# Normalised attention and a snake feed-forward layer on one core: norm steps re-placed, the first batch re-staged, the rest key tile in array quadrants, last stores split

## The chip, the cores and the metric

One core of one Trainium2 chip runs the whole program. The metric is the device time of one execution in microseconds (us). It is read beside a profile of one execution, whose times are counted from that execution's first instruction.

## The reference

The inputs are q, k and v with 8 batches, 12 heads, 448 tokens and a head dimension of 64, two gains g_q and g_k of length 64, and a feed-forward layer with w_in (768 x 2048), w_out (2048 x 768) and alpha (2048). All are float32.

```python
q_n, k_n = rmsnorm(q, g_q), rmsnorm(k, g_k)          # over the head dimension, eps 1e-6
attn = softmax(q_n @ k_n.T / 8)                       # 448 x 448 for each batch and head
x = (attn @ v), heads side by side                    # 3584 tokens x 768
h = x @ w_in
g = h + sin(alpha * h)**2 / (alpha + 1e-9)
out = g @ w_out                                       # 3584 x 768
```

## The kernel before, in words

**Units of work.** A batch has 6 head pairs, head `hp` with head `hp + 6`, one in partitions 0 to 63 and one in 64 to 127 (`hi` 0 and 1). The index `pi` counts pairs through all batches. Norm works on chunks `ci` of two pairs, three to a batch and 24 in all. The 448 keys make three tiles of 128 and a rest tile of 64 (`t` = 0 to 3).

**Norm of a chunk** (`norm_tasks`, L150 to L223). The steps are: squares of q and k (L165 on ScalarE or L167 on GpSimd), the product of both gains folded into k (`fold_g`, L171), row sums on VectorE (L174), the inverse root by Ln and Exp on ScalarE (L178, L179), the scaling to bfloat16 (L189, L191, L196: five operations), and the transposes. The three chunks of batch 0 are "early": squares on ScalarE, transposes on TensorE into PSUM with a VectorE copy (L212, L213). All others use GpSimd for squares, fold and scaling, and a transposing DMA on SyncE's queue (L202). Only chunk 0 folds and scales on VectorE.

**Attention of a pair.** `scores(pi, t)` (L231) multiplies keys by queries for both heads, which sit in the two row halves of the array, and ScalarE takes the exponential (L243, L245). `attend(pi)` (L247) runs 16 matmuls (L262). For each key tile there are four: values for hi 0 and 1 into PSUM bank 0, and a tile of ones for hi 0 and 1, which gives the softmax sums, into bank 1. hi chooses the column half of the array in both banks; in the rest tile it chooses the row half as well:

```python
r = slice(hi * 64, hi * 64 + 64)
lhsT = vb[b][r, NT * H + hp, :] if bank == 0 else ones[r, :]
nc.tensor.matmul(av[r, bank, :S], lhsT, rhs, start=(t == 0), stop=(t == NT))
```

ScalarE then forms the reciprocal of the sums by Ln and Exp (L264, L265), and one VectorE product writes the pair's rows of xT (L268).

**Feed-forward.** `first_product(b)` (L286) is 16 row tiles of 6 matmuls (L293). The sine follows on ScalarE (L274), its square on GpSimd or ScalarE (L277, L279), and the sum on VectorE (L282). `second_product(b)` (L314) makes units of 16 steps, whose matmuls (L330) end in a VectorE copy (L335) and two stores on SyncE's queue (L340). Its steps are "fillers", run between the attention steps of the next batch; those of batch 7 run at the end.

**Order.** Nothing is reordered by a scheduler: each engine runs its instructions in the order in which Python issues them, and so does each DMA queue. In batch b's pair loop (L377) `bg(n)` (L227) takes the next n entries of the queue `background`, which holds the norm steps of chunks 3b+2 to 3b+4. What is left runs after `first_product` (L415).

**Buffers.** PSUM has four pairs of banks (`bank_pair`) for all products, three q/k chunk buffers (`inp`, L73) and two v buffers exist. `load_qk` (L90) fills a chunk from SyncE's queue, but chunks 1 and 2 come from ScalarE's queue (L116, L117). v, w_in and w_out are loaded with a cast by GpSimd (L104, L109, L140, L146); w_out and the v of batch 1 are issued after pair 2 of batch 0 (L406).

Of the kernel before, what the change touches and what calls it, by code (L numbers as in the profile page):

```python
# [23 lines left out]
BF16 = mybir.dt.bfloat16  # L24
# [7 lines left out]
def kernel(  # L32
# [33 lines left out]
    HALF = D_MODEL // 2  # L66

# [22 lines left out]
    def load_qk(ci, eng=nc.sync):  # L90

        b, dp = ci // NC, ci % NC
        qk[ci] = inp.tile([P, 2, 2 * NJ, D], F32, tag="qk", name="qk")
        for which, src in ((0, q), (1, k)):
            heads = src[b].rearrange("(hi dp pp) (p j) d -> dp (pp p) hi (j d)", hi=2, pp=2, j=NJ)[dp]
            eng.dma_start(out=qk[ci][:, which].rearrange("p (hi j) d -> p hi (j d)", hi=2), in_=heads)

    def load_v(b):


        vb[b] = vpool.tile([P, NT * H + NP, D], BF16, tag="vb", name="vb")
        tok = v[b].rearrange("h (p j) d -> p h (j d)", j=NJ)
        for jj in range(2):
            nc.gpsimd.dma_start(  # L104
                out=vb[b][jj * 64:jj * 64 + 64, :NT * H, :].rearrange("p (h t) d -> p h (t d)", t=NT),
                in_=tok[:, :, jj * NT * D:(jj + 1) * NT * D])
        last = v[b].rearrange("(hi pr) (p j) d -> j hi p pr d", hi=2, j=NJ)[NJ - 1]
        for hi in range(2):
            nc.gpsimd.dma_start(out=vb[b][hi * 64:hi * 64 + 64, NT * H:, :], in_=last[hi])  # L109
# [6 lines left out]
    load_qk(1, nc.scalar)  # L116
    load_qk(2, nc.scalar)  # L117
# [6 lines left out]
    nc.vector.memset(eps, 1e-6)  # L124
    gg = const.tile([P, 1, D], F32)
# [16 lines left out]
    def load_w_out():  # L142
        src = moe_w_out.rearrange("(mt p) d -> p mt d", p=P)
        for half in range(2):
            cols = slice(half * HALF, (half + 1) * HALF)
            nc.gpsimd.dma_start(out=w_out_sb[:, :, cols], in_=src[:, :, cols])  # L146
# [3 lines left out]
    def norm_tasks(ci):  # L150
# [8 lines left out]
        def square(w):  # L159
            if "ms" not in st:  # L160
                st["ms"] = npool.tile([P, 2, 2 * NJ], F32, tag="ms", name="ms")
                st["inv"] = npool.tile([P, 2, 2 * NJ], F32, tag="inv", name="inv")
            st[w] = npool.tile([P, 2 * NJ, D], F32, tag="sq", name="sq")
            if early:
                nc.scalar.activation(st[w], qk[ci][:, w], ACT.Square)  # L165
            else:
                nc.gpsimd.tensor_mul(st[w], qk[ci][:, w], qk[ci][:, w])  # L167

        def fold_g():
            eng = nc.vector if first else nc.gpsimd  # L170
            eng.tensor_mul(qk[ci][:, 1], qk[ci][:, 1], gg.to_broadcast([P, 2 * NJ, D]))  # L171
# [9 lines left out]
        def scale(w):  # L181
            eng = nc.vector if first else nc.gpsimd
# [12 lines left out]
            if w == 1:  # L195
                eng.tensor_mul(n[:, NJ - 1], x[:, :, NJ - 1], inv[:, :, NJ - 1].unsqueeze(2).to_broadcast([P, 2, D]))  # L196
# [18 lines left out]
        none = lambda: None  # L215
        if first:
            return [lambda: (square(0), reduce(0), rsqrt(slice(0, 1)), square(1), scale(0), reduce(1), fold_g(),
                             rsqrt(slice(1, 2)), scale(1)), lambda: pe_transpose(0), lambda: pe_transpose(1)]
        if early:
            return [lambda: (square(0), square(1), fold_g()), none, lambda: (reduce(0), reduce(1)), none,  # L220
                    lambda: (rsqrt(slice(0, 2)), scale(0), scale(1)), none, lambda: pe_transpose(0), lambda: pe_transpose(1)]
        return [lambda: (square(0), square(1), fold_g()), none, lambda: reduce(0), lambda: reduce(1),
                lambda: (rsqrt(slice(0, 2)), scale(0), scale(1)), none, none, transpose]  # L223

    background = deque()

    def bg(n):  # L227
        for _ in range(min(n, len(background))):
            background.popleft()()
# [17 lines left out]
    def attend(pi):  # L247

        b, hp = pi // NP, pi % NP
        e = expT[pi]  # L250
        av = bank_pair("av")
        for t in range(NT + 1):
            for bank in range(2):
                for hi in range(2):
                    r = slice(hi * 64, hi * 64 + 64)
                    if t < NT:
# [5 lines left out]
                    nc.tensor.matmul(av[r, bank, :S], lhsT, rhs, start=(t == 0), stop=(t == NT))  # L262
# [5 lines left out]
        nc.vector.tensor_mul(xT[b][:, hp, :], av[:, 0, :S], rec)  # L268
# [17 lines left out]
    def first_product(b):  # L286
# [15 lines left out]
        for i in range(MT // 2):  # L302
# [4 lines left out]
            for m in (2 * i, 2 * i + 1):  # L307
                late.append(snake(b, tiles[i][:, m % 2, :S], m))
                if len(late) > 1:
                    late.popleft()()  # L310
        while late:
            late.popleft()()

    def second_product(b):  # L314
# [5 lines left out]
        units = [(i, (0, 1)) for i in range(NT + odd)] if b else [(i, (h,)) for h in range(2) for i in range(NT)]  # L320
        for i, halves in units:
            st = {}

            def step(m, i=i, halves=halves, st=st):
# [7 lines left out]
                if m == MT - 1:  # L332
# [18 lines left out]

    gate = const.tile([P, 1], F32)
    nc.gpsimd.tensor_copy(gate, qk[0][:, 0, 0, 0:1])
    load_v(0)
    load_w_in()
    for task in norm_tasks(0):
        task()

    def queue_norm(ci):
        tasks = norm_tasks(ci)  # L360
        if ci + 2 < NC * B:
            tasks[0] = lambda t=tasks[0]: (t(), load_qk(ci + 2))
        background.extend(tasks)

    queue_norm(1)
    bg(1)
    FIRST = 16
    for b in range(B):
        if b:
            nc.scalar.preload_act_table_set(EXP_LN)  # L370
            fillers.extend(second_product(b - 1))
        n_fill = len(fillers)
        for ci in range(NC * b + 2, min(NC * b + 5, NC * B)):
            queue_norm(ci)
        if b and b + 1 < B:
            load_v(b + 1)
        for p in range(NP):  # L377
# [16 lines left out]
            bg(1 if b else 2)  # L394
            if p:
                fill(part[2])
                bg(1)
                scores(pi, 2)
                fill(part[3] - part[2])
            else:  # L400
                bg(1)
                scores(pi, 2)
            bg(1)
            fill(part[4] - part[3])
            bg(1)
            if b == 0 and p == 2:  # L406
                load_alpha()
                load_v(1)
                load_w_out()
        fill(len(fillers))  # L410
        attend(b * NP + NP - 1)
        if b == 0:
            nc.vector.reciprocal(inv_alpha_sb, alpha_sb)
        first_product(b)
        bg(len(background))  # L415
# [30 lines left out]
```

## Time and profile before

| | us |
|---|---|
| median of 3 runs | 488.94 |
| their range | 486.53 to 488.96 |
| the profiled execution | 489.04 |
| its span, first to last instruction | 487.2 |
| TensorE busy, share of the span | 447.9, 92% |
| ScalarE (ACT) busy | 343.5, 71% |
| GpSimd (POOL) busy | 290.9, 60% |
| VectorE (DVE) busy | 194.9, 40% |

The profiled execution is 1.84 us longer than its span. Busy time is an average over stages with different limits: batch 0, where data and norms arrive for the first time, the stages between, and the last second product. So the stages are read one by one. In the rows, PE is TensorE's matmuls, PEld its weight loads, SP is SyncE, and a "q" behind an engine is its queue.

### The profile page before, as it was taken

Reading aid. Unit: us, or ns where it says so; the run is one execution under the profiler, and the core shown is the slowest. Engines: PE = TensorE matmul, PEld = TensorE weight load, DVE = VectorE, ACT = ScalarE, POOL = GpSimd, SP = SyncE. Lnnn points to the kernel's source line nnn. Section 1 sums busy time; section 2 is a strip of 40 time slices with the busy share of each in tenths; the row PEclk is TensorE's granted clock in tenths of the full one; section 3 lists DMA queues with packets and bytes.
Section 4 is the critical chain, followed back from the end, with each engine's and each line's share of the span. In section 5 each row is a group of like instructions: output and inputs, shape, how many; then the busy total and the mean of one; then the engine's idle time right before and its main releaser. Section 6 shows DMA issues by size and latency. Waiting matters only on the chain.

```text
span 487.2 us, 7555 instructions
## 1 busy us (share of the span) xinstructions
PE 447.9 (92%) x2900; PEld 213.0 (44%) x2900; DVE 194.9 (40%) x271; ACT 343.5 (71%) x552; POOL 290.9 (60%) x287
## 2 busy tenths in 40 slices
PE   0566599999999999999999999999999999999995
PEld 0222144444544455444544445444544455444563
DVE  2433226343553326343653336343643346213621
ACT  2564668885887768886887768886887778886800
POOL 4439845895487745996487745995497745501400
PEclk9998789999999999999999999999999999999999
DMA  6999990866565560677266560678166330231022
GB/s 212 192 232 190 198 219 1 165 155 158 93 74 133 141 180 4 91 158 170 80 89 146 147 146 2 88 172 163 74 90 145 71 71 1 47 58 32 1 64 65
DMA packets 83251, 55.02 MB, mean 113 GB/s; under 512 B 62096, under 2 KB 79248, under 8 KB 83216
## 3 DMA queue, kind: packets, MB, share of 16 engines
q1 hardware_dynamic: 57968, 40.85, 36.3%
q0 software_dynamic: 23872, 11.80, 19.8%
q10 hardware_dynamic: 1376, 1.90, 1.3%
q8 instruction: 22, 0.36, 0.3%
q14 instruction: 13, 0.11, 0.1%
HBM read 45.69 MB, written 11.01 MB: 116 GB/s over the span
## 4 chain that ended last, share of the span: by engine, by line
PE 82%; POOL 7%; DMA 5%; ACT 2%; DVE 1%; issue 1%; POOLq 0%
PE hps L293 30%; PE ops L330 29%; PE av L262 15%; PE sc L239 6%; DMA vb<-in_v_dram 3%; POOL sq L167 2%; PE sc L241 2%; DMA qk<-in_q_dram 1%; POOL qkn L191 1%; POOL vb L104 1%; POOL qk L171 1%; POOL qkn L189 1%; DMA qkT<-qkn 1%; POOL vb L109 1%; DVE ms L174 1%
## 5 line engine op out<-in xcount | busy, mean ns | idle before, releaser
L330 PE MATMUL ops<-w_out_sb,g_sb 128*128 128x384 bf16 x896 | 161.9, 327 | 0.5 <-DVE g_sb L282 0.5
L243 ACT ACTIVATE expT<-sc 128x896 bf16<-128x896 f32 x144 | 126.2, 912 | 35.3 <-PE sc L239 34.9
L293 PE MATMUL hps<-xT,w_in_sb 128*128 128x448 bf16 x768 | 148.1, 355 | 0.0
L277 POOL TENSOR_TENSOR s<-s 128x448 f32<-128x448 f32 x64 | 59.8, 934 | 114.9 <-ACT s L274 70.5
L330 PEld LDWEIGHTS <-g_sb 128*128 128x128 bf16 x896 | 80.8, 98 | 72.0 <-issue 23.5
L282 DVE SCALAR_TENSOR_TENSOR g_sb<-s,inv_alpha_sb,hps 128x448 bf16<-128x448 f32 x128 | 81.4, 677 | 75.6 <-POOL s L277 75.6
L293 PEld LDWEIGHTS <-w_in_sb 128*128 128x128 bf16 x768 | 74.9, 98 | 72.9 <-issue 5.0
L274 ACT ACTIVATE s<-hps,alpha_sb 128x448 f32<-128x448 f32 x128 | 73.8, 627 | 31.6 <-PE hps L293 31.6
L268 DVE TENSOR_TENSOR xT<-av,rec 128x448 bf16<-128x448 f32 x48 | 30.0, 625 | 138.7 <-ACT rec L265 138.7
L262 PE MATMUL av<-expT,vb 128*64 128x448 bf16 (+1 forms) x384 | 74.2, 379 | 8.3 <-ACT expT L243 3.9
L262 PE MATMUL av<-expT,ones 128*64 128x448 bf16 (+1 forms) x384 | 71.8, 368 | 0.0
L167 POOL TENSOR_TENSOR sq<-qk 128x896 f32<-128x896 f32 x42 | 70.1, 1698 | 0.0
L189 POOL TENSOR_TENSOR qkn<-qk,inv 128x448 bf16<-128x448 f32 x46 | 42.2, 939 | 39.7 <-ACT inv L179 35.2
L174 DVE TENSOR_REDUCE ms<-sq 128x14 f32<-128x896 f32 x48 | 51.1, 1081 | 26.9 <-POOL sq L167 26.7
L171 POOL TENSOR_TENSOR qk<-qk,gg 128x896 f32<-128x896 f32 x23 | 48.1, 2090 | 11.2 <-ACT sq L165 5.8
L239 PE MATMUL sc<-qkT 64*128 64x448 bf16 x288 | 46.3, 371 | 6.2 <-ACT expT L243 3.3
L264 ACT ACTIVATE rec<-av 128x448 f32<-128x448 f32 x48 | 26.1, 544 | 33.3 <-PE av L262 33.2
L262 PEld LDWEIGHTS <-vb 128*64 128x64 bf16 (+1 forms) x384 | 22.4, 111 | 53.0 <-issue 43.9
L335 DVE COPY osb<-ops 128x768 f32<-128x768 f32 (+1 forms) x31 | 27.2, 877 | 32.6 <-PE ops L330 30.3
L279 ACT ACTIVATE s<-s 128x448 f32<-128x448 f32 x64 | 36.9, 576 | 2.0
L191 POOL TENSOR_TENSOR qkn<-qk,inv 128x384 bf16<-128x384 f32 x46 | 37.2, 831 | 0.0
L265 ACT ACTIVATE rec<-rec 128x448 f32<-128x448 f32 x48 | 27.7, 576 | 1.5
(34 smaller groups left out, 176.2 us busy)
## 6 DMA issues: line engine op xcount, KB each, us to landing
qk<-in_q_dram SPq DMA_DIRECT2D x22, 448.0 KB, 4.7
qk<-in_k_dram SPq DMA_DIRECT2D x22, 448.0 KB, 5.0
out_dram<-osb SPq DMA_DIRECT2D x50, 192.0 KB, 2.7
vb<-in_v_dram POOLq DMA_DIRECT2D x16, 288.0 KB, 5.4
w_in_sb<-in_moe_w_in_dram POOLq DMA_DIRECT2D x2, 1536.0 KB, 28.7
w_out_sb<-in_moe_w_out_dram POOLq DMA_DIRECT2D x2, 1536.0 KB, 24.1
out_dram<-osb SPq DMA_DIRECT2D x12, 96.0 KB, 4.2
qk<-in_q_dram ACTq DMA_DIRECT2D x2, 448.0 KB, 9.8
```

What stands on the lines that cost most here:

```text
L167: nc.gpsimd.tensor_mul(st[w], qk[ci][:, w], qk[ci][:, w])
L171: eng.tensor_mul(qk[ci][:, 1], qk[ci][:, 1], gg.to_broadcast([P, 2 * NJ, D]))
L174: nc.vector.reduce_sum(st["ms"][:, w, :], st[w], axis=AX.X)
L189: eng.tensor_mul(n[:, :, hi, :], x[:, hi], inv[:, hi].unsqueeze(2).to_broadcast([P, NJ, D]))
L239: nc.tensor.matmul(sc[:, hi, :S], kt[r, t * P:(t + 1) * P], qt[r, :], start=True, stop=True)
L243: nc.scalar.activation(expT[pi][:, 2 * t:2 * t + 2, :], sc[:, :, :S], ACT.Exp, scale=SCALE)
L262: nc.tensor.matmul(av[r, bank, :S], lhsT, rhs, start=(t == 0), stop=(t == NT))
L274: nc.scalar.activation(s1, hps, ACT.Sin, scale=alpha_sb[:, m, :])
L277: nc.gpsimd.tensor_mul(s2, s1, s1)
L282: nc.vector.scalar_tensor_tensor(g_sb[:, m, (b % 2) * S:(b % 2 + 1) * S], s2, inv_alpha_sb[:, m, :], hps, op0=ALU.mult, op1=ALU.add)
L293: nc.tensor.matmul(ps[:, m % 2, :S], w_in_sb[:, kt, m * P:(m + 1) * P], x[:, kt, :], start=(kt == 0), stop=(kt == KT - 1))
L330: nc.tensor.matmul(st["ps"][:, k, :HALF], lhsT, w_out_sb[:, m, half * HALF:(half + 1) * HALF], start=(m == 0), stop=(m == MT - 1))
```

## The change

**Norms by table.** The queue `background` is gone. Chunk 3b+5 begins beside `first_product(b)` (`beside_h`: squares, fold and sums after its tiles 1 to 7) and ends at the start of batch b+1 (inverse root and scaling ahead of the pair loop, transposes in slot 2). Chunks 3b+3 and 3b+4 are placed in slots 2 to 18 of the pair loop of batch b, four slots to a pair, and the four DMAs of v follow one to a slot.

**First batch.** All q/k loads go on SyncE's queue, w_in waits for chunk 1's k, chunk 2's squares move from ScalarE to GpSimd, and the folds and scalings of chunks 1 and 2 move from GpSimd to VectorE. The batch has a loop of its own with its steps written out, and dummy matmuls on zeros: 28 at the start, 6 ahead of the first transposes, 4 in each pair. GpSimd issues w_out and the v of batch 1 behind chunk 2's squares alone.

**Rest tile.** In bank 1, head hi now goes to the other column half, in all four key tiles. The sums of a head therefore lie in the other partition half, and the product L268 becomes two, one for each half.

**Last stores.** Batch 7's last unit is split into its two column halves, and one of each two stores of batch 7 goes on ScalarE's queue.

```diff
+    BUSY = (28, 6, 4)
...
-    load_qk(1, nc.scalar)
-    load_qk(2, nc.scalar)
+    load_qk(1)
+    load_qk(2)
...
+    def keep_busy(n, rhs):
+        ps = bank_pair("ps")
+        for _ in range(n):
+            nc.tensor.matmul(ps[:, 0, :rhs.shape[-1]], blank[:, :P], rhs, start=True, stop=True)
...
-            if early:
+            if ci < NC - 1:
                 nc.scalar.activation(st[w], qk[ci][:, w], ACT.Square)
...
-            eng = nc.vector if first else nc.gpsimd
+            eng = nc.vector if early else nc.gpsimd
...
+                    o = r if bank == 0 else slice(64 - hi * 64, 128 - hi * 64)
...
-                    nc.tensor.matmul(av[r, bank, :S], lhsT, rhs, start=(t == 0), stop=(t == NT))
+                    nc.tensor.matmul(av[o, bank, :S], lhsT, rhs, start=(t == 0), stop=(t == NT))
...
-        nc.vector.tensor_mul(xT[b][:, hp, :], av[:, 0, :S], rec)
+        for hi in range(2):
+            r, o = slice(hi * 64, hi * 64 + 64), slice(64 - hi * 64, 128 - hi * 64)
+            nc.vector.tensor_mul(xT[b][r, hp, :], av[r, 0, :S], rec[o, :])
...
+            for task in beside.get(i, ()):
+                task()
...
+        if b == B - 1:
+            units[-1:] = [(NT + odd - 1, (h,)) for h in range(2)]
...
-                        nc.sync.dma_start(out=dst[:, cols], in_=o[jj * 64:jj * 64 + 64, :])
+                        eng = nc.scalar if b == B - 1 and jj else nc.sync
+                        eng.dma_start(out=dst[:, cols], in_=o[jj * 64:jj * 64 + 64, :])
...
+    keep_busy(BUSY[0], blank)
...
+    nc.gpsimd.tensor_copy(gate, qk[1][:, 1, 0, 0:1])
     load_w_in()
...
+    norm[1][0]()
+    norm[1][1]()
+    for p in range(NP):
+        for t in (0, 1, 3, 2):
+            scores(p, t)
+        if p == 2:
+            norm[2][2]()
+        if p == 5:
+            step_of(NC + 1, 5, 6)()
+        if p in (1, 3):
+            norm[p // 2 + 1][3]()
+        if p == 3:
+            step_of(NC, 3, 4)()
+            begin_norm(NC + 1)
+            step_of(NC + 1, 0, 1)()
+        if p:
+            attend(p - 1)
+        keep_busy(BUSY[2], blank)
+        if p == 0:
+            norm[1][2]()
+            load_qk(NC)
+            norm[2][0]()
+        if p == 1:
+            norm[2][1]()
+            load_qk(NC + 1)
+        if p == 2:
+            begin_norm(NC)
+            load_w_out(0)
+            load_alpha()
+            for part in load_v(1):
+                part()
+            load_w_out(1)
+            step_of(NC, 0, 1, 2)()
+        if p == 3:
+            step_of(NC, 5, 6)()
+            step_of(NC + 1, 2)()
+        if p == 4:
+            step_of(NC + 1, 3, 4)()
+    attend(NP - 1)
+    nc.vector.reciprocal(inv_alpha_sb, alpha_sb)
+    first_product(0, beside_h(0))
```

In the loop, step numbers of chunks 1 and 2 mean 0 squares, 1 sums, 2 fold, inverse root and scaling, 3 transposes; of later chunks 0 and 1 squares, 2 fold, 3 and 4 sums, 5 inverse root and scaling, 6 transposes. `begin_norm(ci)` also loads chunk ci+2.

## Rows read from the trace of the kernel before

**Rows 1.** Stages: PE, PEld, DVE, ACT, POOL busy us (instructions), granted clock, DMA share, GB/s.

```profile
16.64:62.27 45.63, 27.97 (x199) 11.42 (x198) 13.49 (x17) 26.46 (x44) 32.25 (x33) 0.85 1.28 206
62.27:82.04 19.77, 19.77 (x98) 9.90 (x99) 8.95 (x15) 14.22 (x25) 7.69 (x9) 0.93 0.67 121
82.04:117.58 35.54, 33.77 (x241) 14.85 (x240) 14.79 (x21) 28.01 (x44) 30.00 (x27) 1.00 0.69 152
174.36:192.62 18.26, 18.26 (x97) 9.43 (x98) 8.74 (x14) 14.22 (x24) 6.77 (x8) 1.00 0.41 98
192.62:225.94 33.32, 33.32 (x242) 14.62 (x240) 14.38 (x18) 27.99 (x44) 30.02 (x27) 1.00 0.67 128
481.75:487.20 5.45, 0.00 (x0) 0.00 (x0) 0.96 (x1) 0.00 (x0) 0.00 (x0) 0.80 0.28 72
```

**Rows 2.** Timeline of ScalarE in batch 0: start, us, instruction, idle before and releaser.

```profile
26.37 0.54 ACT L264 ACTIVATE rec<-av 128x448 f32<-128x448 f32 x1 [4.70 <-PE av L262]
...
47.70 0.32 ACT L178 ACTIVATE inv<-ms,eps 128x28 f32<-128x28 f32 x1 [2.95 <-DVE ms L174]
```

**Rows 3.** The chain of waits in batch 0, in order of time: start, us.

```profile
9.19 16.15 DMA vb<-in_v_dram
...
40.89 2.32 POOL w_out_sb L146 x2
```

**Rows 4.** The tile of w_in in the first 70 us: issues, landing.

```profile
L140 POOL DMA_DIRECT2D w_in_sb<-in_moe_w_in_dram x2: 697/702/707, 9.8 to 10.5; - x2
...
DMA to landing us min/median/max: 24.5/28.7/32.9
```

**Rows 5.** Timeline of SyncE's queue from 23.9 us.

```profile
24.36 0.46 SPq L96 DMA_DIRECT2D qk<-in_k_dram  x1
```

**Rows 6.** DMA issues from 24.36 us: size, us to landing (k of chunk 4).

```profile
qk<-in_k_dram SPq DMA_DIRECT2D x1, 448.0 KB, 18.9
```

**Rows 7.** Groups of instructions, shapes apart: busy us, mean ns of one, idle before.

```profile
L167 POOL TENSOR_TENSOR sq<-qk 128x896 f32<-128x896 f32 x42 | 70.1, 1698 | 0.0
...
L174 DVE TENSOR_REDUCE ms<-sq 128x14 f32<-128x896 f32 x48 | 51.1, 1081 | 26.9 <-POOL sq L167 26.7
...
L171 POOL TENSOR_TENSOR qk<-qk,gg 128x896 f32<-128x896 f32 x23 | 48.1, 2090 | 11.2 <-ACT sq L165 5.8 <-DVE qkn L196 3.7
...
L268 DVE TENSOR_TENSOR xT<-av,rec 128x448 bf16<-128x448 f32 x48 | 30.0, 625 | 138.7 <-ACT rec L265 138.7
...
L165 ACT ACTIVATE sq<-qk 128x896 f32<-128x896 f32 x6 | 5.4, 938 | 0.0
...
L335 DVE COPY osb<-ops 128x384 f32<-128x384 f32 x6 | 3.3, 554 | 1.8 <-PE ops L330 1.8
...
L189 DVE TENSOR_TENSOR qkn<-qk,inv 128x448 bf16<-128x448 f32 x2 | 1.2, 621 | 0.6 <-ACT inv L179 0.6
...
L171 DVE TENSOR_TENSOR qk<-qk,gg 128x896 f32<-128x896 f32 x1 | 1.1, 1083 | 0.0
```

**Rows 8.** Timeline: the rest tile of one attend in batch 3, and its neighbours.

```profile
200.79 0.38 PE L262 MATMUL av<-expT,vb 64*64 64x448 bf16 x2
200.82 0.11 PEld L262 LDWEIGHTS <-ones 64*64 64x64 bf16 x2
201.01 0.35 PE L262 MATMUL av<-expT,ones 64*64 64x448 bf16 x2
...
201.20 0.35 PE L241 MATMUL sc<-qkT 64*64 64x448 bf16 x2
```

**Rows 9.** Timeline: two pairs of attend matmuls in batch 0.

```profile
52.19 0.59 PE L262 MATMUL av<-expT,ones 128*64 128x448 bf16 x2
...
52.56 0.59 PE L262 MATMUL av<-expT,vb 128*64 128x448 bf16 x2
```

**Rows 10.** The tile of the output copies from 440 us: stores, landing.

```profile
L340 SPq DMA_DIRECT2D out_dram<-osb x10: 466/528/589, 441.9 to 483.3; - x10
...
DMA to landing us min/median/max: 2.6/2.6/2.7
```

More of the change, by code (lines that the diff above doesn't have):

```diff
@@ L124 @@
     nc.vector.memset(eps, 1e-6)
+    blank = const.tile([P, 512], BF16)
+    nc.vector.memset(blank, 0.0)
     gg = const.tile([P, 1, D], F32)
@@ L181, in scale @@
         def scale(w):
-            eng = nc.vector if first else nc.gpsimd
+            eng = nc.vector if early else nc.gpsimd
             if "n" not in st:
@@ L284, in snake, with first_product @@
         return finish
-    def first_product(b):
+    def first_product(b, beside):
         x = xT[b]
@@ L349, in fill @@
             fillers.popleft()()
+    keep_busy(BUSY[0], blank)
     gate = const.tile([P, 1], F32)
     nc.gpsimd.tensor_copy(gate, qk[0][:, 0, 0, 0:1])
-    load_v(0)
+    for part in load_v(0):
+        part()
+    nc.gpsimd.tensor_copy(gate, qk[1][:, 1, 0, 0:1])
     load_w_in()
-    for task in norm_tasks(0):
+    norm = {ci: norm_tasks(ci) for ci in range(NC)}
+    for task in norm[0]:
         task()
[L359 to L363, printed above, removed]
@@ L365, with begin_norm @@
-    queue_norm(1)
-    bg(1)
-    FIRST = 16
[L368 to L371, printed above, removed]
-        n_fill = len(fillers)
[L373 to L376, printed above, removed]
+    def begin_norm(ci):
+        norm[ci] = norm_tasks(ci)
+        if ci + 2 < NC * B and ci != NC + 2:
+            load_qk(ci + 2)
@@ new lines, in step_of, with beside_h @@
+    def step_of(ci, *steps):
+        return lambda: [norm[ci][n]() for n in steps]
+    def beside_h(b):
+        ci = NC * b + 5
+        if ci >= NC * B:
+            return {}
+        return {0: [lambda: begin_norm(ci)], 1: [step_of(ci, 0)], 3: [step_of(ci, 1)], 4: [step_of(ci, 3)],
+                5: [step_of(ci, 2)], 7: [step_of(ci, 4)]}
+    FIRST = 16
+    norm[1][0]()
[28 more added lines that the diff above has]
+            for part in load_v(1):
+                part()
+            load_w_out(1)
[5 more added lines that the diff above has]
+            step_of(NC + 1, 3, 4)()
@@ new lines, with beside_e @@
+    attend(NP - 1)
+    nc.vector.reciprocal(inv_alpha_sb, alpha_sb)
+    first_product(0, beside_h(0))
+    for b in range(1, B):
+        nc.scalar.preload_act_table_set(EXP_LN)
+        fillers.extend(second_product(b - 1))
+        n_fill = len(fillers)
+        at = [[] for _ in range(4 * NP + 8)]
+        s0, ci = 2, NC * b + 2
+        if b == 1:
+            load_qk(ci + 2)
+        step_of(ci, 5)()
+        at[s0].append(step_of(ci, 6))
+        if b + 1 < B:
+            for ci in (NC * b + 3, NC * b + 4):
+                at[s0] += [lambda ci=ci: begin_norm(ci), step_of(ci, 0, 1, 2)]
+                for n, step in ((4, 3), (5, 4), (6, 5), (8, 6)):
+                    at[s0 + n].append(step_of(ci, step))
+                s0 += 8
+            for n, part in enumerate(load_v(b + 1)):
+                at[s0 - 1 + n].append(part)
+        def beside_e(slot):
+            for task in at[slot]:
+                task()
@@ L400 @@
             else:
-                bg(1)
+                beside_e(4 * p + 1)
                 scores(pi, 2)
-            bg(1)
+            beside_e(4 * p + 2)
             fill(part[4] - part[3])
[L405 to L409, printed above, removed]
+            beside_e(4 * p + 3)
         fill(len(fillers))
         attend(b * NP + NP - 1)
[L412 to L415, printed above, removed]
+        for slot in range(4 * NP, len(at)):
+            beside_e(slot)
+        first_product(b, beside_h(b))
     for s in second_product(B - 1):
```

44 lines of the change are left out of this document (21 added, 23 removed).

## The prediction

> **What bounds the kernel now.** I read the busy times by stage first, because the shares over the span mix stages. From the end of batch 0 on, TensorE is never idle: in the pair loop of batch 3 it is busy for all of 33.32 us and in a first product for all of 18.26, at full granted clock [rows 1]. There only fewer or shorter matmuls can help. Batch 0 is different. From its first exponential at 16.64 to its first product at 62.27 us, 45.63 us pass, in which GpSimd works 32.25 us, TensorE 27.97 (at a mean granted clock of 0.85), ScalarE 26.46 and VectorE 13.49 [rows 1]: they wait for each other. ScalarE's timeline tells for what: 4.70 us for the first attend, 2.95 for VectorE's sums, behind which stands GpSimd [rows 2]. The chain of waits names the causes: the values of batch 0 land only 16.15 us after their last issue, at 25.3 us, and GpSimd spends 2.32 us issuing w_out with the next squares behind it [rows 3]. Batch 1's pair loop takes 35.54 us, 2.2 more than that of batch 3 with as many fillers, and 1.77 of them TensorE stands still [rows 1].
>
> Under all this lies a second limit: in those 45.63 us the DMA engines move 206 GB/s at a share above 1 [rows 1]. The second half of w_in, issued at 10.5, lands 32.9 us later, at 43.4 [rows 4], and chunk 4's k, issued at 24.36, lands 18.9 us later, at 43.3 [rows 5, 6]. While these are asked for no earlier, batch 0 can't end before about 44.
>
> **The change, step by step.** The sum is made against the profiled execution, 489.04 us (span 487.2 and 1.84 around it), which is within 0.1 of the median of 488.94.
>
> *Batch 0.* First exponential: q and k of chunk 0 now come alone at the head of one queue, so the squares can start 1 to 2 us earlier; VectorE's chain after them (two sums of 1.08, the fold 1.08, four scalings of at most 0.62 and a small one [rows 7]) is as long as it was. I put it at 15.1 us instead of 16.64. From there ScalarE's work is the 26.46 us less two squares of 0.94 that go to GpSimd [rows 1, 7]: 24.6 us. So ScalarE alone would be done at 39.7. I then stepped through the new order with these durations and found four waits that stay. Pair 2's scores need chunk 1's scaling and transposes, which VectorE reaches only after its sums: 2.1 us. In pair 3 the product of attend 1 stands on VectorE behind chunk 2's fold and scaling (1.08 and 2.6 us), and holds a PSUM pair that the next scores want: 1.7. Attend 2 follows from it: 1.5. The sums of chunk 4 wait for its squares and these for its k: about 1. With the last attend on TensorE (eight pairs of 0.19 us and the starts around them, 2.2 us) the first product starts at 39.7 + 6.3 + 2.2 = 48.2. [...] The dummies add about 0.9 us of work to a pair and shorten the idle stretches, but the gaps of 1.5 to 2 us stay; I add 1.8 and take **50.0**. That is 12.3 us off. The ends are 44, where w_in lands, and 58, where nothing but the first wait and the w_out wait is gained.
>
> What moves with it: GpSimd now issues w_out and the next v right behind chunk 2's squares, some 20 us earlier than 40.89 [rows 3]. Behind those issues stand chunk 3's squares, two of 1.70 [rows 7], for which VectorE's sums and so attend 2's product wait. On SyncE's queue chunk 5's load waits for chunk 2's buffer, alpha stands behind it, and chunk 6's load waits for chunk 3's scaling with two transposing DMAs behind. alpha may so land after the first product has begun and hold the first sine; four PSUM pairs of 2.28 us each (18.26 / 8 [rows 1]) let TensorE run on for about 9 us, so I cost that at nothing.
>
> *First product of batch 0.* It took 19.77 us at a granted clock of 0.93, later ones 18.26 at 1.00 [rows 1]. With dummies in each pair I take 18.5: **1.3** off, between -1 (alpha late by more than PSUM covers) and 1.5.
>
> *Batch 1.* Chunk 5 is normed beside the first product, and chunks 6 and 7 wait for no backlog. GpSimd there is busy 7.69 of 19.77 us [rows 1], so two squares and a fold (1.70, 1.70 and 2.09 [rows 7]) fit, and the 2.1 us by which one of them can delay a sine's square are less than the three tiles of 2.28 us by which PSUM lets TensorE run ahead. I take 33.3 for 35.54: **2.2** off, between 0 and 2.2. The same placing in batches 2 to 7 costs or gains nothing, since TensorE is never idle there; its cover is these idle shares.
>
> *Rest tile.* Two pairs of 64-row matmuls ran one after the other, 0.22 us from the first to the second and 0.19 to what follows [rows 8]. Four quadrants at once save one slot: 0.19, less 0.02 because the ones' weights begin loading that much later. It counts where TensorE is the bound, in 42 attends of batches 1 to 7: 42 x 0.17 = **7.1** off, between 0 and 8.0 (a loss is the third rival). In the whole tiles the halves now come in the order low, high, high, low; each pair still uses both, so I count nothing. The second product on VectorE adds 0.63 us per attend, 3.8 per pair loop, where VectorE works 14.38 of 33.32 us [rows 1, 7]: hidden. If that cover went, a PSUM pair would come free 0.63 us later.
>
> [...] The row first: the two rest matmuls of one pair write the same PSUM bank from different row halves, and so do the two of L241, yet each pair starts as one and the next comes 0.19 us later [rows 8]. [...]
>
> *Last stores.* TensorE's last matmul is where it was. The stage after it, 5.45 us [rows 1], holds a copy of 0.96 us, two issues in a row of some 0.53 each and 2.6 to landing [rows 10]. The half-width copy takes 0.55 [rows 7] and the second issue goes beside the first: 0.4 + 0.5, **0.9** off, between 0.4 and 1.2; nothing is queued on ScalarE there that the issue could hold.
>
> Sum: 12.3 + 1.3 + 2.2 + 7.1 + 0.9 = 23.8; 489.04 - 23.8 = 465.2, so **465** us.
>
> **The rivals.**
> *The loads hold batch 0.* w_in and w_out now stand without a break in GpSimd's queue while chunks 2 to 4 share one other. Chunk 2's loads, which had ScalarE's queue, stand ahead of chunk 3's and 4's. At a third of the 206 GB/s [rows 1], my estimate of that queue's part, one more load of 448 KB [rows 6] takes 6.7 us. Then chunk 4's k lands at 50, and squares, sums, inverse root and reciprocal (1.7 + 1.1 + 0.5 + 1.1, and the last attend's 2.2) put the first product near 57: 472. For it: the DMA share above 1. Against: chunk 1's and 2's requests start earlier, and the loads needed by then are the same bytes as before.
>
> [...]
>
> *The halves' order breaks the pairs.* If a high half behind a high half kept the following low one from running beside it, the six whole-tile pairs of an attend would take up to 0.19 us more each, 1.14 in all, and 42 of them 48 us: 513, slower than before. It decides from 0.57 us per attend (23.8 / 42). For it: no row has this order. Against: the ones' weights begin loading 0.02 us after the pair before starts [rows 8], so weights don't hold the order.
>
> **How the numbers follow.** My forecast has 0.47, the loads 0.24, the quadrants 0.18, the broken pairs 0.06; 0.05 is for several at once, with batch 0 keeping most of its waits (480 to 490). The forecast's own range is 457 to 470: batch 0 at 44 and full quadrants, or at 54. The loads and the quadrants reach to 472, both together to 479, so the range is 456 to 478. A difference within 0.5% (2.4 us, about what a measurement of this kernel can tell from no change) needs half-broken pairs or a batch 0 that stays: 0.05. Slower: 0.08. Faster: 0.87.
>
> **What the profile would show.** Batch 0's first product would start at 48 to 52 us, the first one last 18.3 to 18.6, batch 1's pair loop near 32.3, later ones 1.0 shorter than before, all four rest matmuls of an attend within 0.05 us of one another, and the stage after the last matmul 4.4 us. [...] I am wrong if the first product starts behind 56, or an attend is not shorter.

## The result, and the profile after

The changed kernel takes **475.28 us** (median of 4 runs, 474.92 to 475.72). The kernel before, timed beside it, takes 488.57 (486.53 to 488.96, 4 runs). The ratio is 0.9737, 95% interval 0.9707 to 0.9766: 13.3 us faster, where 24 had been forecast. The profiled execution took 474.92 us with a span of 473.1, against 487.2 before.

The stages first, as in [rows 1]: batch 0 from its first exponential, its first product, the pair loops of batches 1 and 3, and what follows the last matmul. After the two times come the stage's length, the busy time of PE, PEld, DVE, ACT and POOL with instructions, the granted clock, the DMA share and GB/s.

```profile
18.27:56.86 38.59, 29.73 (x219) 12.19 (x222) 28.50 (x33) 24.81 (x42) 26.18 (x21) 0.78 1.33 220
56.86:75.29 18.43, 18.43 (x98) 9.44 (x99) 10.81 (x18) 14.30 (x24) 13.53 (x14) 1.00 1.30 174
75.29:109.98 34.69, 32.77 (x241) 14.22 (x240) 17.22 (x25) 28.25 (x44) 26.27 (x27) 1.00 0.57 131
184.10:216.62 32.52, 32.32 (x241) 14.29 (x240) 16.79 (x22) 27.93 (x44) 25.94 (x27) 1.00 0.54 119
468.99:473.10 4.11, 0.00 (x0) 0.00 (x0) 0.56 (x1) 0.00 (x0) 0.00 (x0) 0.88 0.18 48
```

Against [rows 1], the first product of batch 0 starts at 56.86 instead of 62.27 (5.4 us less) and lasts 18.43 instead of 19.77 (1.3). Batch 1's loop is 0.85 shorter and batch 3's 0.80, and the end 1.34. The loops of batches 2 to 7 together give 5.2. Start, first product, batch 1, batches 2 to 7 and end sum to the 14.1 us by which the span is shorter. VectorE, which was to take the norms of chunks 1 and 2, is busy 28.50 us of batch 0 instead of 13.49, and the first exponential came not at 15.1 but at 18.27, 1.6 later than before.

VectorE's own timeline tells more than that sum. It shows start, us, instruction; the rows are the folds and scalings of chunks 0, 1 and 2:

```profile
12.50 1.15 DVE L199 TENSOR_TENSOR qkn<-qk,inv 128x448 bf16<-128x448 f32 x2
...
20.05 1.80 DVE L181 TENSOR_TENSOR qk<-qk,gg 128x896 f32<-128x896 f32 x1
21.78 2.63 DVE L199 TENSOR_TENSOR qkn<-qk,inv 128x448 bf16<-128x448 f32 x2
...
33.95 1.80 DVE L181 TENSOR_TENSOR qk<-qk,gg 128x896 f32<-128x896 f32 x1
35.68 4.51 DVE L199 TENSOR_TENSOR qkn<-qk,inv 128x448 bf16<-128x448 f32 x2
```

and GpSimd's over the same stretches:

```profile
19.23 4.17 POOL L177 TENSOR_TENSOR sq<-qk 128x896 f32<-128x896 f32 x2 [5.34 <-DVE ms L184]
...
33.13 1.68 POOL L177 TENSOR_TENSOR sq<-qk 128x896 f32<-128x896 f32 x1 [4.60 <-DVE ms L184]
34.97 2.32 POOL L177 TENSOR_TENSOR sq<-qk 128x896 f32<-128x896 f32 x1 [0.16 <-DMA qk<-in_k_dram]
37.37 2.33 POOL L181 TENSOR_TENSOR qk<-qk,gg 128x896 f32<-128x896 f32 x1
```

The fold took 1.08 us and two scalings 1.2 [rows 7] when GpSimd stood idle, and two scalings still take 1.15 for chunk 0. Beside GpSimd's squares the fold takes 1.80 twice, the two scalings 2.63 and then 4.51, and GpSimd's two squares 4.17 instead of 3.40 [rows 7]. Once GpSimd's products are over, VectorE is back at its old pace: the two scalings of k behind them take 1.01 us in chunks 1 and 2, as in chunk 0 (1.02). On VectorE alone that is 0.72 + 1.48 + 0.72 + 3.36 = 6.3 us, in the one engine on which chunks 1 and 2 wait.

The rest tile of one attend on TensorE, as in [rows 8]:

```profile
85.27 0.38 PE L270 MATMUL av<-expT,vb 64*64 64x448 bf16 x2
85.28 0.11 PEld L270 LDWEIGHTS <-ones 64*64 64x64 bf16 x2
85.28 0.38 PE L270 MATMUL av<-expT,ones 64*64 64x448 bf16 x2
85.48 0.35 PE L247 MATMUL sc<-qkT 64*64 64x448 bf16 x2
```

All four now start within 0.01 us, and the next matmul follows 0.21 later, where it was 0.41.

### The profile page after: what moved, and what is told of

It is laid out like the page before. It is cut to its first block, busy times and chain, and to the rows that moved or that the text cites. A ratio compares the mean times of both kernels' runs of the same rounds, so it can differ in the third digit from the quotient of the medians.

```text
span 473.1 us, 7736 instructions
## 1 busy us (share of the span) xinstructions
PE 451.1 (95%) x2954; PEld 214.1 (45%) x2958; DVE 236.7 (50%) x333; ACT 342.8 (72%) x550; POOL 283.0 (60%) x278
## 4 chain that ended last, share of the span: by engine, by line
PE 81%; DVE 7%; ACT 4%; issue 3%; DMA 2%; POOL 1%; SPq 0%; DVEq 0%; POOLq 0%
PE hps L303 31%; PE ops L344 25%; PE av L270 16%; PE sc L245 6%; DVE ms L184 2%; DMA qk<-in_k_dram 2%; POOL s L287 1%; PE sc L247 1%; ACT expT L249 1%; DVE qkn L199 1%; DVE xT L278 1%; DVE qk L181 1%; PE ps L156 1%; ACT rec L273 1%; DVE osb L349 1%
## 5 line engine op out<-in xcount | busy, mean ns | idle before, releaser
L249 ACT ACTIVATE expT<-sc 128x896 bf16<-128x896 f32 x144 | 126.8, 915 | 32.4 <-PE sc L245 31.2
L278 DVE TENSOR_TENSOR xT<-av,rec 64x448 bf16<-64x448 f32 x96 | 59.7, 622 | 115.1 <-ACT rec L273 114.4
L287 POOL TENSOR_TENSOR s<-s 128x448 f32<-128x448 f32 x64 | 59.5, 935 | 96.4 <-ACT s L284 85.2
L177 POOL TENSOR_TENSOR sq<-qk 128x896 f32<-128x896 f32 x44 | 74.9, 1715 | 15.3 <-DVE ms L184 15.1
L270 PE MATMUL av<-expT,vb 128*64 128x448 bf16 (+1 forms) x384 | 72.4, 372 | 0.6 <-DVE xT L278 0.4
L270 PE MATMUL av<-expT,ones 128*64 128x448 bf16 (+1 forms) x384 | 68.4, 367 | 0.0
L199 POOL TENSOR_TENSOR qkn<-qk,inv 128x448 bf16<-128x448 f32 x42 | 38.5, 938 | 46.0 <-ACT inv L189 46.0
L245 PE MATMUL sc<-qkT 64*128 64x448 bf16 x288 | 45.1, 363 | 3.7 <-ACT expT L249 1.6
L181 POOL TENSOR_TENSOR qk<-qk,gg 128x896 f32<-128x896 f32 x21 | 44.2, 2103 | 1.0
L201 POOL TENSOR_TENSOR qkn<-qk,inv 128x384 bf16<-128x384 f32 x42 | 34.0, 830 | 0.0
```

The lines of the kernel that those rows point to most:

```text
L245: nc.tensor.matmul(sc[:, hi, :S], kt[r, t * P:(t + 1) * P], qt[r, :], start=True, stop=True)
L249: nc.scalar.activation(expT[pi][:, 2 * t:2 * t + 2, :], sc[:, :, :S], ACT.Exp, scale=SCALE)
L270: nc.tensor.matmul(av[o, bank, :S], lhsT, rhs, start=(t == 0), stop=(t == NT))
L278: nc.vector.tensor_mul(xT[b][r, hp, :], av[r, 0, :S], rec[o, :])
L287: nc.gpsimd.tensor_mul(s2, s1, s1)
```

## The experiments

They ran on three chips, each beside the kernel before (medians of that kernel 486.34, 487.18 and 487.19). So ratios are compared, and 0.001 of ratio is 0.49 us. The changed kernel itself, repeated on the second chip, gave 475.39 us, ratio 0.9759 (0.9734 to 0.9783): the mark for what follows. As each ratio is known to about 0.0025, a difference of two is known to about 1.7 us; smaller ones rest on what the traces show. Traces differ too: in four of them batch 0 is the same (the changed kernel twice, the stores as before, the sum one tile earlier), and there the first exponential comes at 17.58 to 18.27 us and the first product at 56.86 to 57.30. The trace shown above has the latest exponential and the earliest product of the four.

### The rest tile as before

```diff
-                    o = r if bank == 0 else slice(64 - hi * 64, 128 - hi * 64)
+                    o = r
-        for hi in range(2): ...
+        nc.vector.tensor_mul(xT[b][:, hp, :], av[:, 0, :S], rec)
```

> The changed kernel with the rest tile's halves and the two VectorE products as before. Theory (the four rest matmuls of an attend run at once and save one slot, and the second VectorE product costs nothing): an attend takes 1.75 us again instead of 1.57, 42 attends of batches 1 to 7 give 7.6 us and batch 0 up to 0.9 more, so 482.9 to 483.8 us against 475.3. Rival (the second product takes back a part, through the PSUM pair that comes free 0.63 us later): batches 3, 5 and 7 lose TensorE's idle 0.2 us each and the time is 481.5 or less.

Measured: 481.09 us, ratio 0.9884 (0.9858 to 0.991), 6.1 us slower than the changed kernel. Its loops of batches 1 and 3, by stage:

```profile
74.01:109.80 35.79, 33.90 (x241) 14.75 (x240) 13.95 (x20) 28.30 (x44) 26.28 (x27) 1.00 0.56 127
185.06:218.55 33.49, 33.37 (x241) 14.66 (x240) 13.59 (x17) 27.98 (x44) 25.90 (x27) 1.00 0.53 118
```

The seven loops are 7.4 us longer, 0.18 for each of 42 attends. The slot is thus worth all of the 0.17 that [rows 8] gave, and nothing is lost to the second VectorE product in the loops. In batch 0 the old form is the better one: the first product starts at 55.73, 1.1 us earlier, which is what makes 6.1 of 7.4. I put that down to the second VectorE product, which stands there between ScalarE's reciprocal and TensorE; it was not tried by itself. I had batch 0 on the wrong side here, and the time lies where the rival had it, though not for the rival's reason. The loops are also 0.2 us longer than those of the kernel before (33.49 against 33.32), which returns below.

### Dummies: none ahead of the first transposes, none at all

```diff
-    BUSY = (28, 6, 4)
+    BUSY = (28, 0, 4)
```

and in a second kernel

```diff
-    BUSY = (28, 6, 4)
+    BUSY = (0, 0, 0)
```

> The changed kernel with the six dummies ahead of the first transposes taken out. Theory (they stand in the way: they run from 13.7 to 16.0 us while chunk 0's scaling is done at 14.8): the transposes start 1.2 us earlier, the first exponential is at 17.1 instead of 18.3, and the time is 474.1 us. Rival A (the clock: without them the scores and transposes run slower and give it back): first exponential at 18 or later, 475 to 476. Rival B (what follows hides it, since VectorE and the loads set batch 0's pace): first exponential earlier, but the first product still at 56.5 to 57.

> The changed kernel without any dummy matmul. Theory (the dummies hold TensorE's clock up in part of batch 0, and batch 0 is set by VectorE's chain, in which TensorE's work has a part): more attends of batch 0 at 0.37 us per pair, first product 2 to 4 us later, first product longer by up to 1.3 us: 477 to 480 us. Rival (the dummies only take TensorE time, the clock falls in the same places): 473.5 to 475.3 us and the same mean granted clock, 0.78 from the first exponential to the first product.

Measured: 472.96 us, ratio 0.972 (0.9692 to 0.9748), without the six: 1.9 better than the changed kernel. And 473.08, ratio 0.9727 (0.9701 to 0.9753), without any: 1.6 better, where I had expected a loss. The cause of the first is in TensorE's timeline of the changed kernel: six dummies wait for the same scaling as the transposes and stand ahead of them.

```profile
13.71 2.40 PE L156 MATMUL ps<-qkn,blank 128*128 128x448 bf16 x6 [4.62 <-DVE qkn L199]
16.03 1.46 PE L222 MATMUL tp<-ident,qkn 64*128 64x64 bf16 x28
```

Without them the transposes begin at 13.60 and the first exponential comes at 16.40, 1.87 earlier than in the trace above and 1.2 to 1.9 earlier than in the four. Without any dummy, batch 0 and its first product read, by stage:

```profile
16.38:55.10 38.72, 26.82 (x199) 11.42 (x198) 28.08 (x32) 24.22 (x42) 25.02 (x20) 0.74 1.29 229
55.10:74.30 19.20, 18.22 (x97) 9.30 (x96) 11.28 (x18) 14.62 (x25) 14.28 (x15) 1.00 1.36 153
```

The granted clock is lower, 0.74 against 0.82 over the same stretch with the 28 and the 4 per pair kept, and yet the first product starts at 55.10 against 54.91. This doesn't show that the clock costs nothing. The chain of waits has attend 3 in both kernels (start, us). With the four dummies per pair, 28 at the start and no six:

```profile
46.60 1.57 PE av L270 x16
48.16 0.97 PE ps L156 x4
```

and without any dummy:

```profile
46.49 2.82 PE av L270 x16
```

In the changed kernel an attend took 1.57 us at a granted clock of 1.00 (from 48.54) and another 2.93 at 0.50 (from 26.53); without dummies the clock over 45 to 50 us was 0.66. So I put it down to the clock that the attend takes 1.25 us more, and the four dummies that no longer stand behind it give 0.97 back. The rest of the price comes later. The first product runs at 1.00 in both kernels, but without dummies TensorE stands 0.98 us in it for the last VectorE products:

```profile
56.88 5.46 PE L303 MATMUL hps<-xT,w_in_sb 128*128 128x448 bf16 x28 [0.98 <-DVE xT L278]
```

The chain of that wait leads back through chunk 4's sums on VectorE to the same slow attend. Read so, the clock does cost something here, and it nearly cancels against the dummies' own time. The profiled execution without dummies took 474.13 us, 1.05 above the median of its four, so the others may not have had that last wait.

### GpSimd held until VectorE has scaled

Two small GpSimd copies, each of one column of the scaled chunk, let the squares of chunks 2 and 3 begin only when the scalings of chunks 1 and 2 are done:

```diff
+            scaled[ci] = st["n"]
...
+            nc.gpsimd.tensor_copy(gate, scaled[1][:, 1, NJ - 1, 0, 0:1])
             norm[2][0]()
...
+            nc.gpsimd.tensor_copy(gate, scaled[2][:, 1, NJ - 1, 0, 0:1])
             step_of(NC, 0, 1, 2)()
```

> The changed kernel with two more waits on GpSimd: chunk 2's squares start only when chunk 1 is scaled, chunk 3's only when chunk 2 is. Theory (VectorE's folds and scalings read two tiles and are held up by GpSimd reading at the same time: 1.80 us instead of 1.08 for a fold, 2.63 and 4.51 instead of 1.16 for the first two scalings of chunks 1 and 2): they fall back to 1.08 and 1.16, chunk 2's transposes start 5 us earlier, the first product starts at 52 instead of 56.9 and the time is 470 to 471 us. Rival A (the loads slow VectorE's reads, not GpSimd): the durations stay, and the time is 475 to 477. Rival B (the squares are then too late for VectorE's sums): the durations fall, but the sums of chunks 2 or 3 wait for GpSimd and the first product stays at 55 to 57.

Measured: 469.88 us (467.54 to 470.74), ratio 0.965 (0.9613 to 0.9686), 5.3 better than the changed kernel. VectorE's timeline, the same rows as above for chunks 1 and 2 (left out: what lies between the chunks):

```profile
19.91 1.08 DVE L182 TENSOR_TENSOR qk<-qk,gg 128x896 f32<-128x896 f32 x1
21.59 1.16 DVE L200 TENSOR_TENSOR qkn<-qk,inv 128x448 bf16<-128x448 f32 x2 [0.60 <-ACT inv L190]
...
30.62 1.08 DVE L182 TENSOR_TENSOR qk<-qk,gg 128x896 f32<-128x896 f32 x1
31.62 1.16 DVE L200 TENSOR_TENSOR qkn<-qk,inv 128x448 bf16<-128x448 f32 x2
```

GpSimd's squares are back to 3.31 for two. Nothing but the start of GpSimd's work was moved, and to a later time, and the first product starts 7.5 us earlier, at 49.39. Batch 0 from its first exponential, by stage:

```profile
18.14:49.39 31.25, 26.95 (x222) 10.89 (x221) 22.28 (x33) 24.90 (x42) 22.23 (x21) 0.89 1.20 237
```

The loads were not what slowed VectorE (rival A): the DMA engines move 237 GB/s here, more than the 220 in the changed kernel. Of the 7.5 us, 6.3 are VectorE's shorter instructions. About 1.3 are TensorE's: on the chain of waits attend 0 takes 1.60 us here, and 2.93 in the changed kernel, at a granted clock of 0.50. The gates themselves uncover the next wait, the one I had costed at nothing. ScalarE's timeline:

```profile
55.33 1.28 ACT L286 ACT_TABLE_LOAD   x1 [4.64 <-DMA alpha_sb<-in_moe_alpha_dram]
```

The first sine waits 4.64 us for alpha, and the first product lasts 19.31 instead of 18.43.

### The gates, and alpha early on ScalarE's queue

```diff
-        nc.sync.dma_start(out=alpha_sb, in_=moe_alpha.rearrange(...))
+        nc.scalar.dma_start(out=alpha_sb, in_=moe_alpha.rearrange(...))
...
     norm[1][0]()
     norm[1][1]()
+    load_alpha()
...
-            load_alpha()
```

> The kernel with the two gates on GpSimd and alpha loaded from ScalarE's queue right after chunk 1's squares, instead of behind chunk 5 on SyncE's. Theory (with the gates the first product starts at 49 us but its first sine waits 4.6 us for alpha, which stalls TensorE when its four PSUM pairs are full): the wait is gone, the first product lasts 18.4 us again and the time is 2 to 4 us below the kernel with the gates alone. Rival (alpha's small packets hold up the loads of chunks 2 to 4 by as much as is gained): the squares of chunks 2 to 4 start later, and the time is the same within 1 us.

Measured: 467.59 us (467.45 to 467.87), ratio 0.9603 (0.9584 to 0.9622), 2.3 below the gates alone and 7.6 below the changed kernel. The first product starts at 49.40 and lasts 18.50, and no instruction waits for alpha. Issued so early, its 8 KB still needed 31.2 us to land, beside the big loads.

### The norms of chunks 1 and 2 back on GpSimd

```diff
-            eng = nc.vector if early else nc.gpsimd
+            eng = nc.vector if first else nc.gpsimd
```

> The changed kernel with folds and scalings of chunks 1 and 2 on GpSimd again. Theory (VectorE held up by GpSimd is no faster than GpSimd alone, 5.7 and 7.6 us per chunk against 6.0, but GpSimd's queue gets longer, and w_out's issue and chunk 3's squares stand behind it): chunk 3's sums end some 4 us later, first product at 59 to 61, the time 3 to 4 us above the changed kernel. Rival A (moving them to VectorE was itself the gain of batch 0): first product at 62 or later, 5 us or more above. Rival B (VectorE's load was the limit): it gets faster than the changed kernel.

Measured: 477.78 us, ratio 0.9815 (0.9793 to 0.9837), 2.7 slower than the changed kernel. The first product starts at 59.64. Even stretched, VectorE's norms are the better place: on GpSimd they delay w_out's issue to 38.30 and chunk 3's squares to 43.44. Moving these norms to VectorE was thus worth 2.8 us at the first product, even with the stretching.

### The sum beside the first product one tile earlier

```diff
-                5: [step_of(ci, 2)], 7: [step_of(ci, 4)]}
+                5: [step_of(ci, 2)], 6: [step_of(ci, 4)]}
```

> The changed kernel with the second sum of chunk 3b+5 issued beside tile 6 of the first product instead of tile 7. Theory (behind tile 7 it stands between the last two sums of the snake on VectorE, and the first fillers wait for the last one: 1.25 us in batch 1, some 0.1 in batches 2 to 7): batch 1's pair loop 1.2 us shorter, 34.7 to 33.5, the time 1.2 to 2 us below the changed kernel. Rival (batch 1's wait comes from GpSimd's late square of the sine, not from the sum): the wait stays, and the time is within 0.5 us of the changed kernel.

Measured: 473.72 us, ratio 0.9729 (0.971 to 0.975), 1.5 better. The six loops of batches 2 to 7 lose 0.18 us each (32.51 to 32.34, 37.57 to 37.39), which is the 0.2 by which the loops without quadrants were longer than before: VectorE's sums of 1.08 us each stood ahead of the last sum of the feed-forward, for which the first filler waits. Batch 1 hardly answers (34.69 to 34.63), so its wait has another cause, as the rival had it; there I was wrong.

### No norm beside the first product

All three chunks' steps in the pair loop, eight slots to each, and v in slots 17 to 20:

```diff
     def beside_h(b): ...
+        return {}
...
+            for ci in [NC * b + 2] + ([NC * b + 3, NC * b + 4] if b + 1 < B else []):
+                at[s0] += [lambda ci=ci: begin_norm(ci), step_of(ci, 0, 1, 2)]
+                for n, step in ((4, 3), (5, 4), (6, 5), (8, 6)):
+                    at[s0 + n].append(step_of(ci, step))
+                s0 += 8
```

> The changed kernel with nothing beside the first product: chunk 3b+2 is normed whole in batch b's pair loop, ahead of chunks 3b+3 and 3b+4, eight slots each, as the kernel before spread them. Theory (in batches 2 to 7 TensorE is never idle, so where the steps stand costs nothing; beside the first product they even cost the 0.1 to 0.2 us that the last sum holds up): loops of batches 2 to 7 at 37.4 and 32.4 us, batch 1's within 1 us of the changed kernel's 34.7, the time 0 to 2 us below the changed kernel. Rival (the table's early start is what keeps GpSimd from falling behind): batch 1's loop is 36 us or longer and TensorE idles in later loops, 2 us or more above.

Measured: 488.82 us (10 runs, 487.06 to 490.21), ratio 1.0027 (1.0009 to 1.0045): 13 us slower than the changed kernel, where I expected the same or up to 2 us less. GpSimd's timeline at the end of batch 1's loop, and TensorE's in the first product behind it:

```profile
115.78 1.86 POOL L199 TENSOR_TENSOR qkn<-qk,inv 128x448 bf16<-128x448 f32 x2
117.57 1.62 POOL L201 TENSOR_TENSOR qkn<-qk,inv 128x384 bf16<-128x384 f32 x2
119.50 1.81 POOL L287 TENSOR_TENSOR s<-s 128x448 f32<-128x448 f32 x2
```

```profile
121.79 2.43 PE L303 MATMUL hps<-xT,w_in_sb 128*128 128x448 bf16 x12 [1.63 <-DVE g_sb L292]
```

The third chunk's scaling doesn't fit into the loop and runs on into the first product, ahead of the first sine's square (L287). The sums wait for that, and TensorE for the sums. This happens in three first products, those of batches 1, 3 and 5. More is lost in pair loops, where scores wait for the transposes of a chunk whose norm comes late. TensorE's waits in the whole run (us in all, times, longest):

```profile
PE sc L245 <- DMA qkT<-qkn: 8.5, 5, 2.8
PE hps L303 <- DVE g_sb L292: 5.2, 3, 1.8
```

This isn't the order before, which ran what was left behind the first product (L415), so the 13 us are not what the new placing saved. They show that GpSimd is close to the bound in a pair loop: it was busy 30.02 of 33.32 us before [rows 1], and moving a chunk beside the first product makes that 25.94 of 32.52.

### The last stores as before

```diff
-        if b == B - 1:
-            units[-1:] = [(NT + odd - 1, (h,)) for h in range(2)]
...
-                        eng = nc.scalar if b == B - 1 and jj else nc.sync
+                        eng = nc.sync
```

> The changed kernel with batch 7's last unit whole again and both stores on SyncE's queue. Theory (the half-width copy saves 0.40 us and the second issue goes beside the first): the stage after TensorE's last matmul is 5.4 us again instead of 4.1, and the time is 1.0 to 1.4 us above the changed kernel. Rival (the last store's landing is set by the DMA, whatever the copy and the queue): the stage is 4.1 to 4.5 us and the time the same.

Measured: 476.64 us, ratio 0.9773 (0.9751 to 0.9794), 0.7 slower by ratio and 1.25 by medians. The stage after the last matmul is 5.40 us with a copy of 0.96, against 4.11 and 0.56: 1.3 in the profile.

### The best of it together

The gates, alpha on ScalarE's queue and the sum beside tile 6, by the diffs above, without the six dummies; a second kernel has BUSY = (0, 0, 0), so no dummy at all:

```diff
-    BUSY = (28, 6, 4)
+    BUSY = (28, 0, 4)
```

> The two gates on GpSimd, alpha from ScalarE's queue, the second sum beside tile 6, and no dummies ahead of the first transposes. Theory (the four act on different waits and add up: 7.8 us for gates and alpha, 1.7 for the sum, 1.0 to 1.7 for the dummies): 464 to 465.5 us on a chip where the changed kernel takes 475.4. Rival (the next limit, loads of chunks 3 and 4 or GpSimd's queue in the first product, takes back what the earlier start gains): first product at 47.5 us or earlier, but the time 466 or above.

> As the one before, without any dummy. Theory (the dummies of each pair hold the clock in the now shorter batch 0, whose mean granted clock with the gates is 0.94 against 0.78): without them attends of batch 0 fall back to 0.37 us per pair and the first product starts 1 to 3 us later: 465.5 to 468 us. Rival (they only take TensorE's time): the same within 0.5 us.

Measured: **466.17 us** (466.03 to 466.62), ratio 0.9566 (0.955 to 0.9582), with 28 and 4 dummies. That beats both kernels, the one before by 4.3% and the changed one by 2.0%. Without any dummy it is 467.25, ratio 0.9586 (0.9566 to 0.9605). The stages of the first kernel, batch 0, its first product and batch 1's loop:

```profile
16.00:49.58 33.58, 28.05 (x225) 11.08 (x222) 22.81 (x34) 24.91 (x42) 22.81 (x21) 0.87 1.20 225
49.58:68.01 18.43, 18.43 (x98) 9.45 (x99) 10.73 (x18) 14.30 (x24) 15.74 (x16) 1.00 1.45 176
68.01:102.27 34.26, 32.94 (x241) 14.23 (x240) 17.16 (x25) 28.25 (x44) 25.87 (x27) 1.00 0.93 171
```

This misses the 464 to 465.5 that I expected. The first exponential is at 16.40 again, but the first product starts at 49.58, no earlier than with gates and six dummies (49.40): these two gains don't add. The chain of waits names the next limit (start, us):

```profile
9.39 16.52 DMA vb<-in_v_dram
```

The values of batch 0 land at 25.9, as they did in the kernel before (25.3), and the first attend ends behind them: ScalarE waits 3.32 us for it and starts its reciprocal at 26.38. So here a load does hold batch 0.

Without any dummy the first product starts at 49.2 and then loses 1.0 us in its first tiles waiting for the last VectorE product, as above. I had expected the clock to cost that. The mean granted clock of batch 0 was not lower (0.90 against 0.87), but the chain again leads through a long attend 3:

```profile
40.76 2.75 PE av L272 x11
```

With the dummies it took 1.57. The 1.1 us between the two medians are less than these ratios can tell apart.

## Why the prediction was right and wrong

**Right in direction and range, half the size.** Of 23.8 us, the profile shows 14.1. Batch 0 gave 6.9 less than its term, batch 1's loop 2.4 less (forecast 32.3, measured 34.69), the loops of batches 2 to 7 0.9 less, and the end 0.4 more. The measured 475 lies outside the forecast's own range of 457 to 470. It is inside the stated 456 to 478 only because the rivals on loads and quadrants had widened that, and neither came true: that it fits is luck.

**Batch 0: the step that failed is "I then stepped through the new order with these durations".** They came from [rows 7], where VectorE's folds and scalings ran while GpSimd was idle. The change itself put GpSimd's squares beside them, and there they took 6.3 us longer. This is shown: with the durations restored by the gates and nothing else moved, the first product starts at 49.39, and I had forecast 50.0. That these two are so near is in part luck. With the gates the first exponential still comes at 18.14, 3.0 later than forecast, and the stage from there takes 31.25 us instead of 34.9. ScalarE works 24.90 of them (24.6 forecast). It waits 5.9 before its last step, against 6.3 for the four waits I listed, so those were about right. But I had added 2.2 for the last attend, which ends only 0.43 after ScalarE's last step, and 1.8 for the clock, and neither comes on top. No run shows that term of 1.8; what the traces show is a granted clock of 0.89 over this stage, and in the changed kernel attends of 2.93 us at 0.50 and of 1.57 at 1.00. So batch 0 missed by 3.2 us at its start and 7.3 through the stretched work, and 3.7 that I had counted too much hid a third of it.

**The first exponential, forecast at 15.1, came at 18.27.** Of the 3.2 us, the six dummies are 1.9 in this trace (1.2 to 1.9 over four), shown by leaving them out. I counted the dummies as work that shortens idle stretches, but these six stand in TensorE's queue ahead of the transposes, waiting for the same scaling. The other 1.3 us were only read from the traces and not tried: chunk 0's first squares do start 1.1 us earlier (6.66 against 7.74), but VectorE waits for the gains until 8.36, and the squares of k start at 9.52, when k has landed. VectorE's scaling of k begins at 13.57, where it was 13.69. In the best version this start no longer matters, since there the first attend waits for the values.

**The first product of batch 0**: 18.5 forecast, 18.43 measured. The reason I gave for it, dummies in each pair, is not shown: without them the product also runs at a granted clock of 1.00.

**The rest tile: right.** 0.17 forecast and 0.18 measured per attend, 7.4 us over 42. (The 0.02 in that term is 0.03 in [rows 8], which changes nothing.) The cost of the second VectorE product was "hidden" by VectorE's idle share of [rows 1]. That holds in batches 1 to 7 and not in batch 0, where the product stands between ScalarE's reciprocal and TensorE; the old form was 1.1 us better there.

**"The same placing in batches 2 to 7 costs or gains nothing, since TensorE is never idle there"** failed by 0.18 us in each of six loops. The cover was TensorE's busy share, but the new sum stands on VectorE just where TensorE changes from one product to the next and has no other work.

**Batch 1: the 2.2 us did not come.** [rows 1] showed 1.77 us of idle TensorE, and I took a backlog on GpSimd for its cause. TensorE's own waits in that loop of the kernel before say otherwise: 0.9 for an output copy, 0.5 for the feed-forward's sums, 0.4 for exponentials. In the changed kernel 1.92 us of idle time remain, 1.5 of it for the feed-forward's sums (us in all, times, longest):

```profile
PE ops L344 <- DVE g_sb L292: 1.5, 2, 1.2
```

The trace shows what delays those sums. On GpSimd the fold of chunk 5, which the table put beside the first product, stands ahead of the sine's square, and VectorE waits for the square:

```profile
72.78 2.09 POOL L181 TENSOR_TENSOR qk<-qk,gg 128x896 f32<-128x896 f32 x1
75.81 1.92 DVE L292 SCALAR_TENSOR_TENSOR g_sb<-s,inv_alpha_sb,hps 128x448 bf16<-128x448 f32 x3 [1.67 <-POOL s L287]
```

I had counted that delay of 2.1 us as covered by the tiles by which TensorE runs ahead, but at the end of the product no tiles are left. Later batches have nearly the same delay and lose only 0.1 to 0.2. There a step of the second product takes both column halves of one row tile. In batch 0's it takes one half of two, so TensorE is at the last two row tiles within 2.4 us of the product's end. An earlier sum on VectorE didn't cure it (34.63), and in the best version 1.3 us are left. The fold was not moved, so this cause is read and not tried.

**alpha, costed at nothing**, costs next to nothing in the changed kernel (ScalarE waits 0.26 us for it) only because batch 0 is late. With a first product at 49.4 the first sine waits 4.64 us; TensorE runs on through most of that, as forecast, and stands 0.8 us for the first sums behind it, and the first product lasts 0.9 longer; without the wait the run was 2.3 faster.

**The last stores**: 0.9 forecast, 1.34 in the profile, 0.7 to 1.25 by the runs.

**The rivals.** The loads did not hold batch 0 of the changed kernel (in the best version the values do, as seen above). Chunk 4's k was issued at 26.10 and landed 16.3 us later, at 42.4, before its squares began at 44.87; I had priced it at 50. The DMA list (queue, operation, KB, us to landing):

```profile
qk<-in_k_dram SPq DMA_DIRECT2D x1, 448.0 KB, 16.3
```

The quadrants do overlap (the four matmuls start within 0.01 us), and the halves' order breaks nothing (whole-tile pairs stay 0.19 apart). I had given these three 0.48 together, and a slow batch 0 through VectorE wasn't among them, though "I am wrong if the first product starts behind 56" was its mark, and 56.86 is behind it.

## What to carry to other kernels

When work is moved from one engine to another, take its duration not from a row where the other engine was idle but from one where it runs beside what the new order puts there; where no such row exists, a row for the pair is the first thing to measure. Work that is off the critical path can be worth delaying: holding GpSimd back until VectorE was done made the kernel 5.3 us faster here. And six dummy matmuls that waited for the same data as the first transposes held the first exponential up by 1.2 to 1.9 us.

## What the runs showed of the hardware

VectorE's folds and scalings, products of two tiles, took longer while GpSimd's squares and fold ran: two scalings 1.16 us in the gated kernel, 2.63 and 4.51 in the changed one, a fold 1.08 and 1.80; GpSimd's two squares 3.31 and 4.17. Two row sums on VectorE, which have one input, took 2.08 us in the gated kernel both beside GpSimd's scalings (from 45.23) and while GpSimd only issued DMAs (from 28.63).

Four 64 x 64 matmuls on four quadrants, two from different row halves into each of two PSUM banks, start within 0.01 us, and an attend takes 1.57 us, where it took 1.75 with the rest tile as before.

With a granted clock of 0.74 over batch 0 (no dummies) instead of 0.82 (28 and 4) the first product started 0.2 us later. Behind this small difference stand two larger ones: an attend took 2.82 us instead of 1.57, and dummies of 0.97 per pair were gone. In the changed kernel an attend took 2.93 us at 0.50 and 1.57 at 1.00. A mean clock doesn't tell which attend on the chain of waits ran slow.
